# Twenty-four empty ScalarE instructions in a gap before the copies of the result

## The chip, the cores and the metric

The kernel runs on one core of one Trainium2 chip. The metric is the device time of one execution in microseconds; the median of several runs is quoted. Each run is classed by its time and clock, and only runs of the fast state are compared. The span of a profile is about 1.4 us shorter than the device time (201.4 against 202.84 us in the profiled run of the kernel before).

## The reference, cut to what matters

The program is one decode step of a transformer block: layer norm, attention over a cache of 4096 keys and values in 32 heads, a residual, a second layer norm, and a gated feed-forward part (a GLU with GELU). Only the end concerns us:

```python
def _B_ref(x, w_gate, w_up, w_down):
    g = jnp.einsum("bsd,df->bsf", x, w_gate)
    u = jnp.einsum("bsd,df->bsf", x, w_up)
    h = _gelu(g) * u
    return jnp.einsum("bsf,fd->bsd", h, w_down)
# ... one token: B = S = 1, Dm = 640, Df = 1728
h2 = h + _B_ref(_layernorm(h, axis=-1), B_w_gate, B_w_up, B_w_down)
```

## The kernel before

Each operation is put on one engine's list, with the events that it waits for. An operation that somebody waits for raises its engine's semaphore when it is done. `A`, `V` and `T` put work on ScalarE, VectorE and TensorE. The end of the kernel:

```python
ga = glu(ps_g, wg_sb, range(5), hl, d_wg)
glu(ps_u, wu_sb, range(3), d_wu[0])
up = glu(ps_u, wu_sb, range(3, 5), d_wu[1])
# ... g1, g2, g3: three VectorE steps on the gate
g5 = A(lambda e: e.activation(e_t[:, :], t2[:, :], ACTF.Exp, bias=zero_t[:, 0:1], scale=-2.0 * GELU_C0 * GELU_C1), g3)
# ... g7, g8, g6: three VectorE steps that follow from the exp
g9 = V(lambda e: e.tensor_mul(hm[:, :], gu[:, :], ps_u[:, 0:15]), g6, up)
# ... the down projection on TensorE, as its weights land
dn = {q: T(down([12], [q]), d_wd[3]) for q in (0, 2, 1, 3)}
os = [V(lambda e, q=q: e.tensor_copy(out_row[0:1, 160 * q:160 * q + 160], ps_d[32 * q:32 * q + 1, 0:160]), dn[q])
      for q in range(2)]
os += [A(lambda e, q=q: e.copy(out_row[0:1, 160 * q:160 * q + 160], ps_d[32 * q:32 * q + 1, 0:160]), dn[q])
       for q in range(2, 4)]
d_out = P.dma("sync", out[0, :, :], out_row[:, :], *os)
```

The result is 640 numbers in four quarters; VectorE copies two of them and ScalarE two, side by side, and the store waits for all four. On ScalarE nothing lies between the exp `g5` and its copies.

The softmax here doesn't subtract the row's maximum and nothing guards it: scores larger than these inputs give would overflow.

## Time and profile before

| | before |
|---|---|
| device time, three runs before the prediction | 202.89 us (202.81 to 203.33) |
| span of the profile | 201.4 us |
| ScalarE busy | 12.6 us, 6% of the span |
| ScalarE idle between the exp's end and its copies | 5.89 us |
| last piece of weights in use from | 198.69 us |
| store of the result issued | 200.27 us |

A line of the timeline has start, length, engine, source line, operation and tiles; the brackets give how long the engine was idle before it and what ended that. A q behind an engine's name means its sequencer: the profile files there what an engine's stream does without the part that computes, its datapath, such as waits and the issuing of transfers (on ScalarE before, a wait of 17 ns at 1.8 us and a transfer's issue of 0.50 us at 1.30). The prediction below shows the lines themselves.

### The profile page before, as it was taken

The page shows a single profiled execution, that of the slowest core. Times are in us where ns is not written, and L with a number is a line of the kernel's source. Part 1 is how long each engine was busy: PE and PEld are TensorE (multiplying, and loading weights), DVE is VectorE, ACT ScalarE, POOL GpSimd, SP SyncE. Part 2 cuts the span into 40 slices and gives each one's busy share as a digit, 9 for nine tenths or more (in the row PEclk, how much of TensorE's full clock was granted, in tenths as well). Part 3 has the DMA queues.
Part 4 walks back from the last instruction along what each step waited for, and adds up shares of the span by engine and source line. Part 5 has one row for each costly group of instructions (what it writes and reads, how often), then busy time and mean ns, then how long its engine had stood idle before and what let it go on. Part 6 is the DMA issues. An engine that isn't in the chain of part 4 may idle for free.

```text
span 201.4 us, 2003 instructions
## 1 busy us (share of the span) xinstructions
PE 119.7 (59%) x1009; PEld 33.8 (17%) x756; DVE 100.9 (50%) x51; ACT 12.6 (6%) x33; POOL 34.4 (17%) x36
## 2 busy tenths in 40 slices
PE   0107009659617943696299257907791697678684
PEld 0101000001200020112010201200201012268572
DVE  0200098983598079605970994199209933220321
ACT  2100000001000100010001001000000010010101
POOL 6400000000090018000900350053004400100000
PEclk9999757978966985589769859995599589685555
DMA  9989999999999999999999999999999999999992
GB/s 325 439 387 462 442 429 423 416 423 459 442 429 423 423 423 429 456 436 436 416 423 423 442 442 436 436 423 416 429 449 436 436 429 403 431 419 423 412 410 98
DMA packets 3848, 84.30 MB, mean 419 GB/s; under 512 B 450, under 2 KB 644, under 8 KB 1156
## 3 DMA queue, kind: packets, MB, share of 16 engines
q1 hardware_dynamic: 3842, 84.23, 97.8%
q8 instruction: 4, 0.07, 0.1%
q10 hardware_dynamic: 2, 0.00, 0.0%
HBM read 84.23 MB, written 0.00 MB: 418 GB/s over the span
## 4 chain that ended last, share of the span: by engine, by line
DMA 85%; PE 10%; SPq 4%; issue 0%; DVE 0%
DMA v_slot<-in_A_v_cache_dram 71%; DMA k_slot<-in_B_w_down_dram 13%; PE psum L363 9%; SPq L59 4%; PE psum L516 0%; DVE out_row L525 0%
## 5 line engine op out<-in xcount | busy, mean ns | idle before, releaser
L375 DVE TENSOR_TENSOR prod<-k_slot,qb 128x8192 bf16<-128x8192 bf16 x16 | 75.2, 4736 | 6.1 <-DMA k_slot<-in_A_k_cache_dram 6.1
L167 PE MATMUL psum<-prod,id_b 128*128 128x512 bf16 x233 | 65.0, 434 | 0.0
L381 DVE TENSOR_REDUCE sc<-psum 128x128 f32<-128x2048 f32 x8 | 18.3, 2291 | 50.7 <-PE psum L167 50.7
L385 POOL TENSOR_TENSOR p_bd<-pt,own 128x512 bf16<-128x512 bf16 x6 | 28.3, 4716 | 87.2 <-ACT pt L382 87.2
L352 PE MATMUL psum<-prod,id_b 128*128 128x512 bf16 x23 | 10.4, 452 | 49.4 <-DVE prod L375 46.2
L363 PE MATMUL psum<-v_slot,p_bd 128*16 128x512 bf16 x224 | 18.3, 484 | 7.4 <-DMA v_slot<-in_A_v_cache_dram 7.4
L352 PEld LDWEIGHTS psum<-prod,id_b 128*128 128x128 bf16 x23 | 2.3, 99 | 69.6 <-DVE prod L375 52.2
L369 PEld LDWEIGHTS psum<-hs,po_sb 128*128 128x128 f32 x64 | 8.3, 191 | 24.1 <-issue 23.5
L363 PEld LDWEIGHTS psum<-v_slot,p_bd 128*16 128x16 bf16 x224 | 5.8, 105 | 38.9 <-DMA v_slot<-in_A_v_cache_dram 30.7
L392 ACT COPY po_sb<-psum 128x512 f32<-128x512 f32 x7 | 4.1, 586 | 73.3 <-PE psum L363 73.3
L369 PE MATMUL psum<-hs,po_sb 128*128 128x4 f32 x64 | 7.7, 244 | 0.4 <-ACT po_sb L428 0.4
L382 ACT ACTIVATE pt<-sc,zero_t 128x128 bf16<-128x128 f32 x8 | 3.2, 401 | 70.4 <-DVE sc L381 70.4
L335 PE MATMUL psum<-arena,xlnB 128*32 128x512 bf16 x20 | 3.1, 579 | 7.3 <-DMA arena<-in_A_wq_dram 7.3
L465 PE MATMUL psum<-aP,arena 128*128 128x1 bf16 x160 | 6.7, 178 | 0.7 <-DMA arena<-in_A_wo_dram 0.6
L465 PEld LDWEIGHTS psum<-aP,arena 128*128 128x128 bf16 x160 | 6.6, 131 | 0.9 <-DMA arena<-in_A_wo_dram 0.7
L389 POOL MEMSET spare<- 1x1 f32 x1 | 0.1, 89 | 35.6 <-DVE p_bd L385 35.6
L494 PE MATMUL psum<-hlnT,v_slot 128*128 128x1 bf16 x150 | 5.5, 173 | 0.7 <-issue 0.7
L340 DVE CAST qb<-psum 128x512 bf16<-128x512 f32 x1 | 0.7, 692 | 9.8 <-PE psum L167 9.8
L494 PEld LDWEIGHTS psum<-hlnT,v_slot 128*128 128x128 bf16 x150 | 5.4, 120 | 1.3 <-issue 0.7
L363 PE MATMUL psum<-k_slot,p_bd 128*16 128x512 bf16 x32 | 3.5, 616 | 2.8 <-DVE p_bd L385 2.8
L308 PE MATMUL psum<-one_bf,x_row 1*128 1x1 bf16 x5 | 0.4, 177 | 7.1 <-DMA x_row<-in_A_x_dram 7.1
L311 DVE COPY xx<-psum 128x5 f32<-128x5 f32 x1 | 0.2, 165 | 7.5 <-PE psum L308 7.5
(73 smaller groups left out, 34.2 us busy)
## 6 DMA issues: line engine op xcount, KB each, us to landing
k_slot<-in_A_k_cache_dram SPq DMA_DIRECT2D x8, 4096.0 KB, 26.3
v_slot<-in_A_v_cache_dram SPq DMA_DIRECT2D x7, 4096.0 KB, 17.0
arena<-in_A_wq_dram SPq DMA_DIRECT2D x1, 5120.0 KB, 15.6
arena<-in_A_wo_dram SPq DMA_DIRECT2D x2, 2560.0 KB, 33.7
k_slot<-in_A_v_cache_dram SPq DMA_DIRECT2D x1, 4096.0 KB, 25.2
v_slot<-in_B_w_gate_dram SPq DMA_DIRECT2D x1, 2160.0 KB, 24.7
k_slot<-in_B_w_down_dram SPq DMA_DIRECT2D x3, 640.0 KB, 30.1
v_slot<-in_B_w_up_dram SPq DMA_DIRECT2D x1, 1296.0 KB, 27.4
```

Source lines behind the costliest of these rows:

```text
L59: ev = self.op(eng, lambda e: e.dma_start(out, in_), *deps, dma=True, chan=chan)
L167: built = e.matmul(out, lhsT, rhs, start=start, stop=stop)
L352: mm = held if n or not first else lambda e, *a, **k: e.matmul(*a, **k)
L363: i = e.matmul(ps_o[a:a + 16, :], p_bd[:, 4 * b:4 * b + 4, :].rearrange("p g j -> p (g j)"), vt[:, 4 * b:4 * b + 4, :], start=(b < 4), sto ...
L369: i = e.matmul(ps_a[:, bass.ds(at, 4)], po_sb[:, 128 * r:128 * r + 128], hs[:, r, :], start=(r == 0), stop=(r == 3))
L375: mults[G, i] = VM(lambda e: e.tensor_tensor(out=prod[:, i, :, :], in0=kt[:, 64 * i:64 * i + 64, :], in1=qb[:, G, :].unsqueeze(1).to_broad ...
L381: reds[G] = VR(lambda e: e.reduce_sum(sc[:, :], ps_f.rearrange("p (g d) -> p g d", d=16), axis=AX.X), folds[G, 1])
L382: exps[G] = AS(lambda e: e.activation(pt[:, :], sc[:, :], ACTF.Exp, bias=zero_t[:, 0:1], scale=INV_SQRT_DH, accum_out=RS[:, G:G + 1]), red ...
L385: blocks[G] = on(lambda e: e.tensor_tensor(out=p_bd[:, :, :], in0=pt[:, :].unsqueeze(2).to_broadcast([128, 128, 4]), in1=own[:, :].unsquee ...
L392: evs[G] = AS(lambda e: e.copy(po_sb[:, :], ps_o), pvs[G])
L465: r = e.matmul(ps_p[:, c:c + 1], wo_sb[:, i, c::5], aP[:, i:i + 1], start=False, stop=(i == 31), skip_group_check=True)
L494: i = e.matmul(ps[:, m:m + 1], ws, hlnT[:, c:c + 1], start=(c == 0 and m == 0), stop=(c == 4), skip_group_check=True)
```

## The change

It puts 24 nops, instructions that do nothing, between the exp and the copies in ScalarE's stream. They depend on nothing and signal nobody. The question is what instructions cost when they do nothing, and whether the gap covers that cost.

```diff
     g9 = V(lambda e: e.tensor_mul(hm[:, :], gu[:, :], ps_u[:, 0:15]), g6, up)
 
+    def idle(eng, n):
+
+        def fn(e):
+            for _ in range(n):
+                i = e.nop(hint="n", nofuse=True)
+            return i
+        return P.op(eng, fn)
+    idle("scalar", 24)
+
     def down(ms, qs=range(4)):
```

## The prediction

> **What bounds the kernel now.** I read the chain of waits that ended last first, because it alone says which work sets the end. Its last pieces, whose columns are start in us, length in us, and what:
>
> ```profile
> 171.63 27.02 DMA k_slot<-in_B_w_down_dram
> 198.64 0.04 issue
> 198.69 0.88 PE psum L516 x18
> 199.56 0.30 DVE out_row L525
> 199.86 0.03 issue
> 199.89 0.32 DVE out_row L525
> ```
>
> The chain waits 27 us for a transfer, the last piece of the down projection's weights, and then has little left: 0.88 us of matmuls and two copies of the result on VectorE. ScalarE is not in the chain at all. The page says the same of the whole kernel:
>
> ```profile
> q1 hardware_dynamic: 3842, 84.23, 97.8%
> q8 instruction: 4, 0.07, 0.1%
> ...
> HBM read 84.23 MB, written 0.00 MB: 418 GB/s over the span
> ```
>
> The data queue keeps the 16 transfer engines occupied for 97.8% of the span, so the kernel's time is 84.23 MB of reads at about 418 GB/s (84.23 / 418 = 201.5 us, the span) with a short tail behind the last byte. A change that neither moves bytes nor holds up a transfer's start can act on that tail only.
>
> Next the timeline of the tail (start, length, engine, line, operation; in brackets how long that engine had been idle and what ended it):
>
> ```profile
> 193.18 0.17 DVE L503 SCALAR_TENSOR_TENSOR t<-t,g_t 128x15 f32<-128x15 f32 x1
> 193.39 0.31 ACT L505 ACTIVATE e_t<-t,zero_t 128x15 f32<-128x15 f32 x1 [4.21 <-DVE t L503]
> 193.73 0.17 DVE L506 TENSOR_SCALAR t<-e_t 128x15 f32<-128x15 f32 x1 [0.37 <-ACT e_t L505]
> ...
> 196.26 0.17 DVE L509 TENSOR_TENSOR hm<-gu,psum 128x15 bf16<-128x15 f32 x1 [1.86 <-PE psum L494]
> ...
> 198.69 0.83 PE L516 MATMUL psum<-k_slot,hm 128*1 128x160 bf16 x20 [0.61 <-DMA k_slot<-in_B_w_down_dram]
> 199.55 0.66 DVE L525 CAST out_row<-psum 1x160 bf16<-1x160 f32 x2 [3.12 <-PE psum L516]
> 199.59 0.60 ACT L527 CAST out_row<-psum 1x160 bf16<-1x160 f32 x2 [5.89 <-PE psum L516]
> 200.27 0.27 SPq L59 DMA_DIRECT2D out_dram<-out_row  x1
> ```
>
> The reader should see three times here. ScalarE's exp ends at 193.39 + 0.31 = 193.70. Its next work, two copies of the result, starts at 199.59, when the matmuls release it: 5.89 us of idleness, in which the new instructions are put. And ScalarE's two copies end at 199.59 + 0.60 = 200.19, VectorE's two at 199.55 + 0.66 = 200.21, so ScalarE has only about 0.02 us to spare in the copies themselves: once the empty instructions outlast the gap, nearly all of the excess goes to the end.
>
> Last I looked for any wait that ScalarE's sequencer handles by itself, in the view of the line that issues waits:
>
> ```profile
> L114 SPq EVENT_SEMAPHORE  x2: 17/17/17, 200.2 to 201.4; - x2
> L114 ACTq EVENT_SEMAPHORE  x1: 17/17/17, 1.8 to 1.8; - x1
> ```
>
> There is one on ScalarE's sequencer, at 1.8 us, and none later. All later waits are carried by the engine instructions themselves. And one line of the timeline of the start shows the sequencer going on while its engine is busy:
>
> ```profile
> 1.27 1.28 ACT L249 ACT_TABLE_LOAD   x1 [1.27 <-PEq L546]
> 1.30 0.50 ACTq L59 DMA_DIRECT2D x_row<-in_A_x_dram  x1
> ```
>
> The table load occupies ScalarE until 2.55, and the sequencer issues the transfer behind it at 1.30.
>
> [...]
>
> **The change part by part.** It removes nothing and moves nothing. It adds 24 nops to ScalarE's stream, between the exp and the copies, in program order. They have no dependency, write no tile and signal nobody. No semaphore count changes, so every other engine's program and waits stay as they are.
>
> Cost of one. [...]the pieces called issue in the chain, between back-to-back instructions of a sequencer, are 0.03 to 0.06 us. So I estimate 0.05 + 0.017, some 0.07 us for each. A coarser check from the end: the last ScalarE copy ends at 200.19, VectorE's at 200.21, and the store is issued at 200.27; in those 0.06 us a wait passed through SyncE's sequencer and the next instruction began. The sum is 24 x 0.07 = 1.7 us, with 24 x 0.03 = 0.7 us and 24 x 0.1 = 2.4 us as a generous frame.
>
> What of it lies on the path. There are two cases, and neither puts any of it there. If the sequencer were held at the exp until it starts, the nops would run from 193.39 or, held until it ends, from 193.70 to 193.70 + 1.7 = 195.4, and the copies would be dispatched 4.2 us before their matmuls are done at 199.5. If, as I expect, [...] the sequencer passes on, they run much earlier. [...] The choice between the two I make by the table load; the time doesn't depend on it. The exp itself stands ahead of the nops and can't be delayed by them, so the GLU's VectorE steps at 193.73 to 194.39 stay, and even they have slack: the multiplication at 196.26 waits for the up projection's matmuls, not for the exp's branch. Sum on the path: 0.00 us. 202.89 + 0.00 = 202.9.
>
> **The rivals.** First, nops that are dear and in order. To reach the copies they must take 5.89 / 24 = 0.245 us each, counted from the exp's end. At 0.3 us each it would be 7.2 - 5.9 = 1.3 us late, so 204.2; to be 2% slower, 4.06 us, they need (5.89 + 4.06) / 24 = 0.41 us. The 17 ns of the wait rows and the issue pieces of 0.04 us speak against it; that no nop is in the trace leaves it open. A weight of 2%.
>
> Second, an additional instruction fetch. [...] In the records of single packets, those four took 1.02 to 1.10 us each. [...] such a packet could delay the end by up to about 1.1 us: 204.0. [...]
>
> Third, the nops change when the final copies are dispatched[...]. [...] ScalarE's start at 199.59, 0.04 us after VectorE's, is a reaction to the matmul's signal. I give it 0.05 us either way.
>
> Fourth, TensorE's own stream. Before the last 6 matmuls of the up projection and again before the down projection the profile names issue as what ended the waits (0.67 and 0.26 us). TensorE's program gets no instruction, so these stay; and the wait for the transfer at 198.69 covers changes of some tenths there.
>
> **Range and chances.** What remains is spread: the three runs of before lie between 202.81 and 203.33, and the new runs may be on another chip [...]. I take 202.4 to 203.5 as the range that should hold it 8 times in 10: 0.5 us below, as nothing is removed and the fastest run was 202.81, and 0.6 above, for the spread's upper end with a little for the second rival. Faster by over 2% would need under 198.8, for which I see no mechanism: 1%. Slower by over 2% needs over 206.9, which only the first rival gives: 2%. Within 2%: 97%.
>
> **What would show each step right or wrong.** The changed profile should show the nops on ScalarE's sequencer 24 times, with starts 0.03 to 0.1 us apart, [...] not after 193.70; the exp starting the same 0.2 us after VectorE's step; ScalarE's copies starting 0.03 to 0.05 us after VectorE's; the last piece of down weights still ending the chain's long wait; the instruction queue at 4 packets. Wrong would be: nops that reach beyond 199.5, copies of ScalarE that start with issue as their releaser instead of the matmuls, a fifth instruction packet with a longer wait for the weights, or TensorE's stalls grown.

The sum is 202.89 + 0.00 = 202.9 us: nothing on the path, and 24 x 0.07 = 1.7 us off it, in ScalarE's gap. Passages that no trace or run of this case shows are cut where marked: what stood behind the 0.017 us, which is also the 17 ns of the wait rows, and behind the issue pieces; how long before the exp the nops would run if they passed it; where the copies wait before 199.5; and how the second rival's fetch would come about, and its chance. That rival's 1.1 us is the estimate from the four packets' 1.02 to 1.10 us; that such a packet can hold up the weights was not shown.

## The result, and the profile after

| | before | after |
|---|---|---|
| device time, four runs each | 203.07 us (202.81 to 203.33) | 202.80 us (202.73 to 202.87) |
| ratio to before | | 0.9986, 95% interval 0.9969 to 1.0004 |
| span of the profile | 201.4 us | 201.4 us |

A ratio is the mean time of one kernel's fast runs over that of the other's of the same rounds, so it isn't quite the ratio of the medians. The interval holds 1: the change made no difference that could be seen.

The timeline of after, the lines that answer to those of before:

```profile
193.30 0.31 ACT L505 ACTIVATE e_t<-t,zero_t 128x15 f32<-128x15 f32 x1 [4.21 <-DVE t L503]
...
196.14 0.17 DVE L509 TENSOR_TENSOR hm<-gu,psum 128x15 bf16<-128x15 f32 x1 [1.83 <-PE psum L494]
...
199.47 0.66 DVE L534 CAST out_row<-psum 1x160 bf16<-1x160 f32 x2 [3.16 <-PE psum L525]
199.51 0.60 ACT L536 CAST out_row<-psum 1x160 bf16<-1x160 f32 x2 [5.90 <-PE psum L525]
200.19 0.27 SPq L59 DMA_DIRECT2D out_dram<-out_row  x1
```

ScalarE's datapath is idle for 5.90 us before the copies, as before (5.89), and still the matmuls are what end it. The copies start 0.04 us after VectorE's, also as before. The last pieces of the chain that ended last:

```profile
171.39 27.18 DMA k_slot<-in_B_w_down_dram
198.56 0.04 issue
198.61 0.87 PE psum L525 x20
199.48 0.30 DVE out_row L534
...
```

It passes through the same transfer, matmuls and VectorE copies. Where the nops went is told by the view of their source line (count, then shortest, median and longest length in ns, then the first and last start in us):

```profile
L515 ACTq NOP  x24: 14/14/14, 193.3 to 194.2; - x24
```

They are on the sequencer (ACTq), 14 ns each as recorded. In the records of single instructions the exp starts at 193.299, the first nop at 193.304 and the last at 194.210; the starts are (194.210 - 193.304) / 23 = 39.4 ns apart. So together they fill 0.92 us of the 6.2 us between the start of the exp and that of the copies.

One thing in the page was not there before:

```profile
q8 instruction: 4, 0.07, 0.1%
q14 instruction: 1, 0.01, 0.0%
```

A fifth packet of instructions, of 8 KB by its record, at 201.25 us. That is 1.06 us after the store of the result was issued.

### The profile page after: what moved, and what is told of

Read it like the earlier page. It is cut to its first block, busy times and chain, and to the rows that moved or that the text cites. A ratio compares the mean times of both kernels' runs of the same rounds, so it can differ in the third digit from the quotient of the medians.

```text
span 201.4 us, 2026 instructions
## 1 busy us (share of the span) xinstructions
PE 118.0 (59%) x1008; PEld 33.4 (17%) x756; DVE 100.9 (50%) x51; ACT 12.6 (6%) x33; POOL 34.6 (17%) x36
## 4 chain that ended last, share of the span: by engine, by line
DMA 85%; PE 9%; SPq 4%; issue 0%; DVE 0%
DMA v_slot<-in_A_v_cache_dram 71%; DMA k_slot<-in_B_w_down_dram 13%; PE psum L363 9%; SPq L59 4%; PE psum L525 0%; DVE out_row L534 0%
## 5 line engine op out<-in xcount | busy, mean ns | idle before, releaser
L363 PE MATMUL psum<-v_slot,p_bd 128*16 128x512 bf16 x224 | 17.8, 474 | 7.0 <-DMA v_slot<-in_A_v_cache_dram 7.0
```

Of the source, the lines that this page charges most:

```text
L363: i = e.matmul(ps_o[a:a + 16, :], p_bd[:, 4 * b:4 * b + 4, :].rearrange("p g j -> p (g j)"), vt[:, 4 * b:4 * b + 4, :], start=(b < 4), sto ...
```

## The experiments

Theory A: ScalarE's sequencer handles the nops in order, held by the wait of the exp ahead of them, and spends 39 ns on each; they cost the kernel nothing until they outlast the moment when the matmuls release the copies. The main rivals: a cost that is there but too small to see with 24 (B), an end that absorbs any delay since transfers bound the kernel (C), and a cost of fetching the additional instructions (D). Two batches of four kernels each ran, each on one chip with its own eleven runs of the kernel before: median 202.99 us (202.75 to 203.55) in the first, and 202.93 us (202.86 to 203.50) in the second. All eight kernels gave correct results.

### 120 nops

```diff
-    idle("scalar", 24)
+    idle("scalar", 120)
```

> 120 nops in the place of 24. Theory A (the sequencer is held by the exp's wait, then spends 39 ns on each nop, as the trace of the changed kernel shows): the nops end at about 193.3 + 120 x 0.039 = 198.0 us, still 1.5 us before the matmuls release the copies, so the time stays at 202.9 us (within 0.3). Rival B (the gap's apparent slack is not real, and each nop costs the end something): 24 nops cost under 0.3 us, so 120 could cost up to 1.5 us, 204.4 us.

Measured: 202.90 us (202.76 to 202.95), ratio 0.9995 (0.998 to 1.001).

```profile
L515 ACTq NOP  x120: 14/14/14, 193.4 to 198.4; - x120
```

Five times as many cost nothing that can be seen either: the interval leaves 0.2 us for all 120 together, where rival B had up to 1.5, so it falls. The last nop starts at 198.4, some 0.3 us later than the count times 39 ns gives from this run's start of the exp (193.44 + 119 x 0.0392 = 198.1). The next run shows why. The fifth packet of instructions came at 197.73 us here, while the last weights were still on their way, and they landed at 198.70, against 198.65 before and 198.57 with 24 nops.

### 240 nops

```diff
-    idle("scalar", 24)
+    idle("scalar", 240)
```

> 240 nops, more than the gap holds. Theory A: they end at about 193.3 + 240 x 0.0392 = 202.7 us, the copies of ScalarE start right after with no wait for the matmuls, 3.2 us later than before, so the time is about 206.1 us (205.7 to 206.5). Rival C (the kernel is bound by transfers and the end absorbs it): 202.9 us. Rival D (240 more instructions also need an additional fetch of instructions, which holds ScalarE): another packet in the instruction queues and some 1 to 2 us more than theory A, 207 to 208 us.

Measured: 206.87 us (206.73 to 207.05), ratio 1.0195 (1.0179 to 1.0211): 3.9 us slower, clear of noise, though the interval leaves open whether it is more than 2%. The timeline:

```profile
199.66 0.66 DVE L534 CAST out_row<-psum 1x160 bf16<-1x160 f32 x2 [3.25 <-PE psum L525]
203.48 0.59 ACT L536 CAST out_row<-psum 1x160 bf16<-1x160 f32 x2 [9.71 <-issue]
204.16 0.27 SPq L59 DMA_DIRECT2D out_dram<-out_row  x1
```

VectorE's copies are where they were, ScalarE's come 3.8 us after them, and what ends ScalarE's idleness is now called issue: it was waiting for nothing but its own stream. Rival C falls: nothing absorbs a late copy. But 3.9 us is more than the 3.2 of theory A, and 206.87 lies above its range. The chain of waits around 194.5 us has the reason:

```profile
194.49 0.01 ACTq L515
194.50 0.03 issue
194.53 0.01 ACTq L515
194.54 0.33 issue
194.87 0.01 ACTq L515
194.88 0.03 issue
```

The usual step between two nops is 0.03 us of issue and 0.01 of nop. Once it is 0.33 and 0.01, and a second time at 199.86, where the issue piece is 0.32. In the records these come after the 28th and the 156th nop, 128 instructions apart. The page has two packets where the run of 120 had one:

```profile
q14 instruction: 2, 0.02, 0.0%
```

Their records show 8 KB each, and starts at 197.65 and 200.82, so 3.1 and 1.0 us after the two steps began. The steps are 0.30 and 0.29 us longer than usual by the records, and 3.2 + 0.59 = 3.8, close to the 3.9 measured. Rival D is right that a further packet comes and that the time is above theory A's 206.1, by 0.8 us and not by 1 to 2; that fetching is what costs it is not shown. The packets start after the steps are over and the sequencer has gone on (its next nop is at 194.87 after the first step and at 200.18 after the second), so the step isn't a wait for these packets; what the sequencer does in it, no run shows. What is shown is that the step has its place in the stream: two later runs have it after the 16th nop, where twelve other instructions stand ahead of the nops (12 + 16 = 28), and after the 29th, where the nops start one place earlier.

### The same 24 nops between the two copies

```diff
-    idle("scalar", 24)
...
+    for q in range(2, 4):
+        os.append(A(lambda e, q=q: e.copy(...), dn[q]))   # the same copy as before
+        if q == 2:
+            idle("scalar", 24)
```

> The same 24 nops moved between ScalarE's two copies of the result, where there is no gap. Theory A: they start with the first copy, at about 199.51, and end 24 x 0.0392 = 0.94 us later at 200.45; the second copy starts then in place of 199.82, so the output's store is issued some 0.6 us later: 203.5 us (203.3 to 203.7). Rival C (nops cost nothing because the engine's datapath does not see them): 202.9 us.

Measured: 203.60 us (203.52 to 203.65), ratio 1.0029 (1.0017 to 1.0041), so 0.6 us slower.

```profile
199.73 0.28 ACT L536 CAST out_row<-psum 1x160 bf16<-1x160 f32 x1 [5.90 <-PE psum L524]
200.69 0.29 ACT L536 CAST out_row<-psum 1x160 bf16<-1x160 f32 x1 [0.68 <-issue]
201.07 0.27 SPq L59 DMA_DIRECT2D out_dram<-out_row  x1
```

The two copies used to follow each other after 0.31 us; now the second starts 0.96 us after the first, released by issue. The 0.65 us between these reach the end. The nops have the price that theory A gives them, and the place alone decides whether it is paid.

### What holds the nops: twelve copies ahead of them

```diff
+    junk = sb("junk", [128, 12, 160], FP32)
+    for n in range(12):
+        A(lambda e, n=n: e.copy(junk[:, n, :], zero_t[:, 0:1].to_broadcast([128, 160])))
     idle("scalar", 24)
```

> Twelve copies of 128 x 160 into a scratch tile, with no wait, go between the exp and the 24 nops, to see what the sequencer waits for. They should take about 0.31 us each, so from 193.6 to about 197.3. If the sequencer only has to dispatch them, the nops start at about 194 us, while the first copies run. [...] If a nop waits until the instruction before it starts, they start at about 197. In all three the nops end before 199.5 and the time stays at 202.9 us (within 0.4).

Measured: 202.99 us, one run. The copies and the nops:

```profile
193.54 0.31 ACT L505 ACTIVATE e_t<-t,zero_t 128x15 f32<-128x15 f32 x1 [4.20 <-DVE t L503]
193.75 2.79 ACT L520 COPY junk<-zero_t 128x160 f32<-128x160 f32 x12
```

```profile
L515 ACTq NOP  x24: 14/14/14, 193.9 to 195.1; - x24
```

The copies overlap and take 0.225 us each from start to start, less than I assumed. By the records the first nop starts at 193.885, when the first copy is running (193.752) and the other eleven haven't started. So nops don't wait for the work ahead of them to start or to finish. The first nop comes 0.35 us after the exp's start and not 5 ns; spread over the twelve copies that is about 29 ns for each (0.347 / 12), an estimate that takes it that the nops keep their place behind the copies. With 24 nops alone, they started 5 ns after the exp, though ScalarE had been idle for 4.21 us before it, so work in progress on ScalarE can't be what held them there. What is left is the exp's own unmet wait, and the next run tests that.

### 120 nops ahead of the GLU's exp

The nops move from behind `g5` to ahead of it.

> 120 nops ahead of the GLU's exp instead of behind it. If it is the wait of the instruction ahead in the stream that holds the nops, they start with the layer norm's second exp at about 188.9, 4.5 us earlier than those behind the GLU's exp, and end at 188.9 + 120 x 0.0392 + 0.31 = 193.9. The GLU's exp then starts some 0.45 us late, released by issue and not by VectorE, and the multiplication that needs it still waits for the up projection's matmuls, as it had 1.6 us to spare: 202.9 us (within 0.3). If the nops could run ahead of waits, they would be done before 188 and the exp would not move.

Measured: 202.95 us (202.90 to 203.03), ratio 0.9998 (0.9984 to 1.0013).

```profile
L509 ACTq NOP  x120: 14/14/14, 188.9 to 193.8; - x120
```

```profile
188.86 0.29 ACT L320 ACTIVATE ln<-ln,zero_t 128x1 f32<-128x1 f32 x1
...
193.15 0.17 DVE L503 SCALAR_TENSOR_TENSOR t<-t,g_t 128x15 f32<-128x15 f32 x1
193.91 0.31 ACT L514 ACTIVATE e_t<-t,zero_t 128x15 f32<-128x15 f32 x1 [4.75 <-DVE t L503]
...
196.31 0.17 DVE L518 TENSOR_TENSOR hm<-gu,psum 128x15 bf16<-128x15 f32 x1 [1.39 <-PE psum L494]
```

The nops start with the instruction that is now ahead of them, the layer norm's exp at 188.86, 4.5 us earlier than behind the other: the place in the stream decides when they run. The GLU's exp starts 0.59 us after its input is done (193.15 + 0.17 = 193.32) in place of 0.04, and the kernel doesn't care, because the multiplication at 196.31 is still released by the up projection's matmuls. One detail was missed: I expected the profile to name issue ahead of the exp, and it names VectorE, whose step had ended 0.59 us before. By the records the last nop starts at 193.846 and the exp at 193.906.

### 150 and 170 nops: the edge of the gap

```diff
-    idle("scalar", 24)
+    idle("scalar", 150)    # and 170 in the other kernel
```

> 150 nops, just what the gap should hold. Theory A with the block term that the runs of 120 and 240 showed (39.2 ns for each nop, and 0.31 us more [...] after the 28th nop and again after the 156th): the last nop ends near 193.4 + 150 x 0.0392 + 0.31 = 199.6 us, within 0.1 us of when the matmuls release the copies, so the time is 202.9 to 203.1 us. If instead the excess began earlier than the records say (an unseen cost before the copies), it is above 203.3.

> 170 nops, 20 more. Theory A with the block term: 20 x 0.0392 + 0.31 for the second crossing = 1.09 us more than with 150, of which about all lies on the path: 204.0 to 204.2 us. Without the block term, from the nops alone (Theory A as first put): 193.4 + 6.66 = 200.1, some 0.4 us late: 203.3 us.

The block term is the long step that the run of 240 showed, 0.30 us after the 28th nop and 0.29 after the 156th; the second crossing is the second of these.

Measured: 150 nops, 203.00 us (202.84 to 203.18), ratio 1.0001 (0.9988 to 1.0014). 170 nops, 204.18 us (204.00 to 206.81), ratio 1.008 (1.0039 to 1.0121). The copies with 150 and with 170:

```profile
199.60 0.60 ACT L536 CAST out_row<-psum 1x160 bf16<-1x160 f32 x2 [5.90 <-PE psum L525]
```

```profile
201.05 0.59 ACT L536 CAST out_row<-psum 1x160 bf16<-1x160 f32 x2 [6.97 <-issue]
```

With 150 the last nop starts at 199.54 and the copy at 199.60, released by the matmuls: the gap is filled to within 0.1 us and nothing is lost. With 20 more the medians differ by 1.18 us, near the 1.09 of the nops and the second long step together, and far from the 0.4 of the nops alone. One run of 170 took 206.81 us with an ordinary granted clock of TensorE (0.784 of full speed); it is counted in the ratio. None of the 22 runs of the kernel before in these two batches did such a thing. That run has no trace, so its cause stays open.

### The same 24 nops on VectorE

```diff
-    idle("scalar", 24)
+    idle("vector", 24)
```

> The same 24 nops in VectorE's stream, between its last GLU multiplication and its copies of the result. They should start with that multiplication, held by its wait until about 196.2, [...] and end at 197.4, with 2 us to spare: 202.9 us (within 0.3). A cost of over 0.14 us each would show as a later start of VectorE's copies.

Measured: 202.91 us (202.84 to 202.99), ratio 0.9996 (0.9982 to 1.0011).

```profile
L515 DVEq NOP  x24: 18/18/18, 196.5 to 198.0; - x24
```

VectorE's nops are 18 ns long and 47 ns apart outside one step of 0.46 us after the seventh, which I had not expected here. They end at 198.0, 0.6 us later than expected and still 1.7 us before VectorE's copies (199.70). VectorE has less room than ScalarE, 3.2 us from the start of the multiplication ahead (196.46) to that of its copies against 6.2, and enough.

## Why the prediction was right or wrong

- **No effect on the time: right.** 202.80 us against the predicted 202.9, in the range. The sum on the path was put at 0.00, and the runs of 120 and 150 show it: 202.90 and 203.00 us.
- **The gap of 5.89 us: nearly right.** It was counted from the exp's end, but the nops start with the exp, so about 6.2 us can be filled: the 150 nops took 6.16 us (193.394 to 199.555 in the records) at no cost. It was seen to close only between 150 and 170 nops. The prediction's threshold of 0.245 us for each of 24 nops stands against a measured 0.039.
- **The cost of one nop: too high.** The term put at 0.07 us measured 0.039, so 0.92 us for 24 in place of 1.7. The piece that was too large is the issue between two instructions, taken as 0.05 us from other instructions in the chain; between nops it is 0.025 (0.039 less the 0.014 recorded). The cost lies in the frame of 0.7 to 2.4 us.
- **Where the nops run: the preferred case was wrong.** The prediction expected the sequencer to pass the waiting exp and to run the nops much earlier, judging by the transfer issued during the table load. They started 5 ns after the exp, at 193.304. The failing step is "the sequencer passes on". The table load was already running (from 1.27 us) when the transfer behind it was issued (1.30), so it showed only that a busy datapath doesn't hold the sequencer; the twelve copies show the same, with the first nop 0.13 us after the start of the first copy (193.885 against 193.752). An unmet wait does hold the nops: the 24 behind the GLU's exp started with it at 193.3, the 120 ahead of it with the instruction that was then ahead of them, at 188.9. By what means it holds them, no run here tells. The prediction had the other case too, and the same time for both, so the right time isn't luck. (Its 4.2 us from 195.4 to 199.5 should read 4.1; nothing rests on it.)
- **The second rival, a further fetch: the packet came, and cost nothing here.** Measured with 240 nops, ScalarE's long steps are 128 instructions apart, and the packets have 8 KB. As 24 nops and two copies are 26 instructions behind the exp and the step comes after 28, the first step would lie just behind the copies (an estimate from these counts), which fits the fifth packet after the store was issued. So no packet met the weights in that run, which had landed at 198.57, 2.7 us before it; in the run of 120 one did (197.73), and they landed at their usual time (198.70), not up to 1.1 us late. The step costs 0.29 to 0.31 us on ScalarE, and inside the gap even that is free, as the same run shows. The exp is the 35th of the 37 records, and the step comes 28 instructions later, after the 63rd; why there, no run shows.
- **The final copies, and TensorE's stream: right.** The copies start 0.04 us after VectorE's in both profiles, and TensorE's pause before its last up-projection matmuls was 0.67 us before and 0.65 after.

## What to carry to other kernels

An instruction's cost is read from its sequencer as well as from its datapath, and the page's busy time shows only the second (ScalarE's is 12.6 us and 33 instructions in both pages, with the nops and without): compare the total with the gap up to the next release, and the same 24 instructions cost nothing in one place and 0.6 us between the two copies. Find out what starts them too: here they start when the last wait ahead of them in the stream is over (5 ns after the exp), even if work ahead of them hasn't started (eleven of the twelve copies; 0.35 us after the exp). Near a gap's edge, count the long steps of the stream with the instructions (0.29 to 0.31 us each, 128 instructions apart with 240 nops on ScalarE), for 20 nops cost 1.2 us when they took in such a step.
